# Fourteen of 32 attention units turn their first scores by transposing DMAs instead of multiplying queries and keys a second time

## The chip, the cores and the metric

The kernel is one program on one core of a Trainium2 chip. The core has TensorE (PE, which multiplies matrices; PEld is its loading of weights), VectorE (DVE), ScalarE (ACT), GpSimd (POOL) and SyncE (SP), which issues all DMAs; 16 DMA engines move the data. The metric is the device time of one execution, as the median of several runs. A change of less than about 0.3% can't be told from none here.

## The reference

Two attention layers over 2048 positions, 1024 columns and 32 heads of 32 are computed from separate inputs, and their outputs are put side by side. The change lies in the first (A), which goes over four segments of 512 positions: causal softmax attention inside a segment, plus a linear memory of the segments before, mixed by a gate.

```python
for s in range(N):
    qs, ks, vs = q[:, :, s], k[:, :, s], v[:, :, s]
    logits = jnp.einsum("bhqd,bhkd->bhqk", qs, ks) * scale + mask
    p = _softmax(logits, axis=-1)
    a_dot = jnp.einsum("bhqk,bhkd->bhqd", p, vs)
    pq = phi(qs)
    num = jnp.einsum("bhld,bhde->bhle", pq, M)
    den = jnp.einsum("bhld,bhd->bhl", pq, z)[..., None] + 1e-6
    o = g * (num / den) + (1.0 - g) * a_dot
    pk = phi(ks)
    M = M + jnp.einsum("bhld,bhle->bhde", pk, vs)
    z = z + jnp.einsum("bhld->bhd", pk)
```

The second layer (B) is a linear attention with two softmaxes as its feature map; the change leaves it as it is.

## The kernel before

**Tiling.** Layer A runs in 32 units, each one segment and one group of four heads (128 columns). `units` lists them: units 0 to 15 hold segments 0 and 1, units 16 to 31 segments 2 and 3. `produce(u)` projects keys and queries of a unit into PSUM (L420), splits them into two fp16 halves and copies these by six DMAs into an operand tile, in the program `st`, in the trace `S` (L872). `attend(u)` computes the attention. `values(u)` makes the values of two units. Numbers are held as a high and a low fp16 half, so most products are three matmuls or a stack of three along the contraction.

**A unit's attention before.** First, `maxima` multiplies queries (as rows) with keys for each head and each block of 128 queries, only up to the diagonal (L939). 16 products of 128 to 512 columns fill ten PSUM banks. DVE adds the causal mask and keeps the maximum of each row in `mt` (L945). These maxima are split into halves (L959, L962), turned by four small matmuls (L967), copied by ACT into rows 96 to 103 of the operand tile (L969), and spread to the other heads by a small DMA (L971). Second, `scores` multiplies keys (as rows) with queries over 104 contraction rows, so that the maximum of each query is subtracted in the product (L1032): 16 products in ten banks again. ACT takes the exponential of a bank at once (L1036), ACT and DVE write the two fp16 halves `ph` (L1038, L1039), and POOL sets to zero what lies above the diagonal (L1045). Third, `pv` multiplies these with the values, 20 short matmuls for each head in one group (L1068), and DVE adds the parts into `oall` (L1072). Last, the sums are divided and scaled into `osum` (L1091), the memory's part is added, PE transposes the result (L1100), ACT copies it to `oT` and a DMA stores it (L1102).

**Around it.** In the same stage, POOL, ACT and DVE prepare the second layer's weights (`fold`, L444 to L527), which are stored by L1127 through the buffers `fo` and `oT`, and other operands are loaded and stored. A kind of transposing DMA is there already: the key features of a unit, 128 x 1024 in fp16, are turned from `pkh` to `pkt` (L896), and in the last stage `kls` to `pt` (L1645).

**What sets the order.** Every operation is recorded with an engine, a planned duration, a priority and its tiles (`Graph.op`). `Graph.run` then places them one by one: it takes the engine that can start first, and there the ready operation of the lowest priority value, moved by a table of random offsets (`NUDGE`). DMAs are planned with a size in KB against one flow (`FLOW`, in KB per us) and a latency. The order of each engine is fixed by that when the program is built; on the chip each engine runs its list in order and waits where an operand is late. SP's list is in order too.

## Time and profile before

| | |
|---|---|
| median of 3 runs | 1672.32 us (1671.3 to 1675.79) |
| profiled execution, its own time | 1674.35 us |
| span of the profiled execution | 1672.4 us |
| PE busy | 1646.9 us (98%) |
| DVE busy | 1362.0 us (81%) |
| ACT busy | 1112.8 us (67%) |
| POOL busy | 1060.1 us (63%) |
| DMA engines | 55.8% of the span on SP's queue, 279.68 MB |

The profile is of one execution. Busy times are unions of an engine's instructions; PE's ends are modelled, so a matmul's length is longer than its step to the next one. In a group's row stand its busy time and the mean of one instruction, then the engine's idle time before them and what ended it. Slices are fortieths of the span, in tenths. The DMA share is the time that packets took, as a share of 16 engines; since packets can overlap on an engine, it can exceed 1.

### The profile page before, as it was taken

The page shows a single profiled execution, that of the slowest core. Times are in us where ns is not written, and L with a number is a line of the kernel's source. Part 1 is how long each engine was busy: PE and PEld are TensorE (multiplying, and loading weights), DVE is VectorE, ACT ScalarE, POOL GpSimd, SP SyncE. Part 2 cuts the span into 40 slices and gives each one's busy share as a digit, 9 for nine tenths or more (in the row PEclk, how much of TensorE's full clock was granted, in tenths as well). Part 3 has the DMA queues.
Part 4 walks back from the last instruction along what each step waited for, and adds up shares of the span by engine and source line. Part 5 has one row for each costly group of instructions (what it writes and reads, how often), then busy time and mean ns, then how long its engine had stood idle before and what let it go on. Part 6 is the DMA issues. An engine that isn't in the chain of part 4 may idle for free.

```text
span 1672.4 us, 35523 instructions
## 1 busy us (share of the span) xinstructions
PE 1646.9 (98%) x12900; PEld 963.9 (58%) x12900; DVE 1362.0 (81%) x3212; ACT 1112.8 (67%) x2044; POOL 1060.1 (63%) x1393
## 2 busy tenths in 40 slices
PE   8999999999999999999999999999999999999999
...
DMA  7745455769456472757467354276556666853311
GB/s 235 234 133 157 139 173 165 211 187 246 120 162 160 131 179 90 189 180 197 154 196 265 121 197 169 89 255 246 179 136 156 166 173 152 216 151 139 120 57 63
DMA packets 265455, 279.68 MB, mean 167 GB/s; under 512 B 162752, under 2 KB 215744, under 8 KB 256704
## 3 DMA queue, kind: packets, MB, share of 16 engines
q1 hardware_dynamic: 265280, 277.42, 55.8%
...
q14 instruction: 74, 0.61, 0.1%
...
## 4 chain that ended last, share of the span: by engine, by line
PE 58%; DVE 7%; ACT 3%; issue 2%; POOL 1%; DMA 0%; POOLq 0%; ACTq 0%; DVEq 0%
PE proj L616 14%; PE proj L420 11%; PE misc L420 10%; PE proj L1717 5%; PE s L616 3%; PE s L1717 2%; PE s L1032 2%; PE s L939 2%; PE pv L1068 2%; PE misc L616 2%; PE pv L1653 1%; PE misc L1717 1%; DVE mx L1318 1%; PE kv L1472 1%; DVE ph L1039 1%
## 5 line engine op out<-in xcount | busy, mean ns | idle before, releaser
L420 PE MATMUL proj<-S,S 128*128 128x512 f16 (+1 forms) x2304 | 496.5, 344 | 0.7 <-ACT S L447 0.2
L420 PEld LDWEIGHTS <-S 128*128 128x128 f16 x3072 | 289.0, 98 | 162.1 <-issue 3.4
L616 PE MATMUL proj<-S,S 128*128 128x512 f16 x1488 | 343.9, 380 | 9.8 <-ACT cs L622 8.3
L616 PEld LDWEIGHTS <-S 128*128 128x128 f16 x1968 | 187.4, 98 | 223.9 <-issue 12.1
L1045 POOL TENSOR_SCALAR_AFFINE_SELECT ph<-ph 128x256 f16<-128x256 f16 (+1 forms) x448 | 193.5, 454 | 111.2 <-DVE ph L1039 96.0
L1039 DVE SCALAR_TENSOR_TENSOR ph<-s,ph 128x512 f16<-128x512 f32 x320 | 208.8, 684 | 51.9 <-ACT ph L1038 47.6
L945 DVE CUSTOM_DVE_ANT_0 s<-s,causal 128x384 f32<-128x384 f32 (+3 forms) x512 | 241.3, 511 | 8.0 <-PE s L939 5.6
L1038 ACT ACTIVATE ph<-s 128x512 f16<-128x512 f32 x320 | 185.5, 647 | 0.7
L420 PE MATMUL misc<-S,ot 128*128 128x512 f16 x768 | 171.0, 379 | 0.0
L1325 ACT ACTIVATE e<-e,sk 128x256 f32<-128x256 f32 x256 | 114.5, 500 | 58.7 <-DVE e L1322 36.4
L420 PEld LDWEIGHTS <-ot 128*128 128x128 f16 x768 | 73.9, 98 | 88.3
L1036 ACT ACTIVATE s<-s,bdl 128x512 f32<-128x512 f32 x160 | 105.8, 702 | 22.0 <-PE s L1032 21.9
L1036 ACT ACTIVATE s<-s,bd 128x512 f32<-128x512 f32 x160 | 103.0, 689 | 23.6 <-PE s L1032 16.0
L1032 PE MATMUL s<-S 104*128 104x512 f16 (+3 forms) x512 | 113.8, 300 | 0.1
L939 PE MATMUL s<-S 96*128 96x512 f16 (+3 forms) x512 | 112.0, 299 | 0.7 <-DVE dm L992 0.3
L420 PE MATMUL proj<-wv,S 128*128 128x256 f16 x768 | 101.4, 273 | 0.0
L1068 PEld LDWEIGHTS <-ph 128*128 128x128 f16 x2560 | 89.0, 96 | 19.6 <-POOL ph L1045 1.3
L1622 POOL TENSOR_TENSOR e<-e,zb 128x512 f32<-128x512 f32 x64 | 84.9, 1340 | 16.6 <-DVE r L1328 13.5
L1068 PE MATMUL pv<-vl,ph 128*128 128x66 f16 (+1 forms) x2560 | 92.6, 184 | 0.6 <-POOL ph L1045 0.6
L1328 DVE TENSOR_REDUCE r<-e 128x32 f32<-128x1024 f32 x64 | 76.7, 1207 | 13.5 <-ACT e L1325 13.4
L616 PE MATMUL s<-S,S 128*128 128x512 f16 x324 | 78.6, 379 | 0.4 <-DVE S L449 0.4
L945 DVE DVE_READ_ACCUMULATOR2_ANT mt<- 128x1 f32 x512 | 72.4, 141 | 0.0
...
## 6 DMA issues: line engine op xcount, KB each, us to landing
S<-h SPq DMA_DIRECT2D x192, 128.0 KB
...
```

Of the source, the lines that this page charges most:

```text
L420: op(PE, dur, lambda c=c, a=a, b=b, lv=lv, rv=rv: nc.tensor.matmul(pv(), lv(), rv(), start=(c == 0 and a + b == 0), stop=(c == n - 1 and a ...
L616: op(PE, 0.2165, lambda n=n, a=a, b=b, lv=lv, rv=rv: nc.tensor.matmul(ps(), lv(), rv(), start=(start and n == 0 and a + b == 0), stop=(n = ...
L939: nc.tensor.matmul(ps()[:, o:o + 128 * i + 128], st()[0:96, 0, h, 128 * i:128 * i + 128], st()[0:96, 1, h, 0:128 * i + 128], start=True, s ...
L945: dve({128: 0.216, 256: 0.381, 384: 0.6, 512: 0.648}[n], lambda h=h, i=i, o=o, n=n: nc.vector.tensor_tensor_reduce(ps()[:, o:o + n], ps()[ ...
L1032: nc.tensor.matmul(ps()[:, o:o + n], st()[0:104, 1, h, 128 * j:128 * j + 128], st()[0:104, 0, h, 128 * j:512], start=True, stop=True)
L1036: act(0.571, lambda: nc.scalar.activation(ps(), ps(), AF.Exp, bias=0.0, scale=bd()[:, 4, i2, 0:1]), r=[(bd, i2)], w=[ps])
L1038: act(0.478, lambda: nc.scalar.activation(ph()[:, 0], ps(), AF.Copy, scale=2.0 ** 14), r=[ps], w=[(ph, 0)])
L1039: dve(0.6, lambda: nc.vector.scalar_tensor_tensor(ph()[:, 1], ps(), 2.0 ** 14, ph()[:, 0], op0=OP.mult, op1=OP.subtract), r=[ps, (ph, 0)], ...
L1045: nc.gpsimd.affine_select(pd, pd, pattern=[[0, n], [1, 128]], compare_op=OP.is_ge, fill=0.0, base=0, channel_multiplier=-1)
L1068: nc.tensor.matmul(ps()[:, i, n0:n1], ph()[:, a, o:o + 128], vl()[:, j, h4 + h, n0:n1], start=(i == 0 and a == 0), stop=(j == min(i, 2)), ...
L1325: op(ACT, 0.41, lambda i=i: nc.scalar.activation(e()[:, 4 * i:4 * i + 4], e()[:, 4 * i:4 * i + 4], AF.Exp, bias=0.0, scale=sk()[:, i:i + 1 ...
L1717: op(PE, 0.2165, lambda n=n, a=a, b=b: nc.tensor.matmul(ps(), v(a)[:, n, :], wform[w]()[:, b, n, :], start=(start and n == 0 and a + b == ...
```

## The change

For the units in `ROWS` (4 to 7, 12 to 15, 20 to 25) `maxima`, the turned maxima and `scores` are left out. In their place, `line` multiplies queries (as rows) with keys once. DVE adds the mask, multiplies by the negative scale of the logits, writes that back to PSUM and keeps the minimum of each row. ACT takes the exponential of each block with that minimum as its bias, so the mask needs no further step. ACT and DVE write the halves `ph`, and a transposing DMA turns both, 128 x 1024, into `pr`. `pvrow` multiplies one row of blocks with the values as soon as its transpose is there, so that a head's 20 matmuls are in up to four groups. A new entry of the bounds tile `bd` holds the negative scale. The other 18 units work as before, but their `ph` alternate between the buffers of `pr` and `ph`. `osum` is dropped: the scaled output is written to the buffer `oT`, in place. `FLOW` goes from 230 to 300, and the planned size of the old transposing DMA from 512 to 300. All of `NUDGE` is other numbers, so the order of every engine is new.

```diff
--- before.py
+++ after.py
@@ -30,6 +30,7 @@
 XS = (("S8", 4), ("S12", 3))
 XE = (("h3", 2), ("h3", 2), ("S15", 3))
 PVB = ((0, 1, 3, 2),)
+ROWS = (4,5,6,7,12,13,14,15,20,21,22,23,24,25)
 WSUB = ("DVE", "DVE", "DVE", "DVE")
 VLAG = 0.6
 XL = (5, -0.2)
@@ -43,22 +44,22 @@
-NUDGE = {0: 820989, 2: 102852, 3: 529656, 4: 266905, 5: 924189, 6: 435410, 9: 911235, 12: 450738, 13: 124130, 14: 669972,
...
+NUDGE = {0: 793787, 4: 392172, 5: 763851, 6: 686148, 8: 659744, 10: 367413, 11: 396531, 13: 340802, 14: 362282, 17: 982556,
...
@@ -112,7 +113,7 @@
            ("PE", "PE"): 0.0, ("POOL", "ACT"): 0.09, ("POOL", "DVE"): 0.08, ("POOL", "PE"): 0.16, ("POOL", "POOL"): 0.1}
 
     GAP, SHARE, WINDOW, filler = 0.5, 0.6, 3.41, None
-    SLACK, LATE, FLOW = 0.4, 1.5, 230.0
+    SLACK, LATE, FLOW = 0.4, 1.5, 300.0
     KEEP = {"proj": 1, "s": 1, "misc": 1, "pv": 1, "kv": 0}
     MOST = {"proj": 3, "s": 3, "misc": 2, "pv": 1, "kv": 4}
 
@@ -735,6 +736,8 @@
             bd()[:, 4, v, 0], ps()[:, v, 0], SCALE * 2.0 ** -12, bd()[:, 3, v, 1], op0=OP.mult, op1=OP.mult), r=[ps], w=w, prio=prio)
         op(DVE, 0.1, lambda: nc.vector.tensor_scalar(
             bd()[:, 5, v, 0], ps()[:, v, 1], 2.0 ** -14, 2.0 ** -14, op0=OP.mult, op1=OP.add), r=[ps], w=w, prio=prio)
+        op(POOL, 0.26, lambda: nc.gpsimd.tensor_scalar(
+            bd()[:, 4, v, 1], bd()[:, 4, v, 0], 1e-25, -1.0, op0=OP.max, op1=OP.mult), w=w, prio=prio)
         op(POOL, 0.18, lambda: nc.gpsimd.tensor_tensor(
             bd()[:, 0, v], xsc[:, s0:s0 + n, 0:1].to_broadcast([128, n, 2]), wgs[:, kk, :, 0][:, None, :].to_broadcast([128, n, 2]), op=OP.mult),
            r=[*((xscs, x) for x in segs), (wgss, (kk, 0)), (wgss, (kk, 1))], w=w, prio=prio)
@@ -795,6 +798,7 @@
             b(4, 0), ps()[:, :, :, 0], SCALE * 2.0 ** -12, b(3, 1), op0=OP.mult, op1=OP.mult), r=[ps], w=w, prio=prio)
         op(DVE, 0.12, lambda: nc.vector.tensor_scalar(
             b(5, 0), ps()[:, :, :, 1], 2.0 ** -14, 2.0 ** -14, op0=OP.mult, op1=OP.add), r=[ps], w=w, prio=prio)
+        op(POOL, 0.26, lambda: nc.gpsimd.tensor_scalar(b(4, 1), b(4, 0), 1e-25, -1.0, op0=OP.max, op1=OP.mult), w=w, prio=prio)
         op(DVE, 0.14, lambda: nc.vector.reciprocal(b(2), b(3)), w=w, prio=prio)
         op(DVE, 0.12, lambda: nc.vector.reciprocal(b(5, 1), b(5, 0)), w=w, prio=prio)
         for x in range(2):
@@ -893,9 +897,9 @@
                 op(POOL, 1.12, lambda p=p, ph=ph: nc.gpsimd.tensor_tensor(ph()[:, 1], p(), ph()[:, 0], op=OP.subtract),
                    r=[p, (ph, 0)], w=[(ph, 1)], prio=E)
                 d["pkt"] = pkt = G.buf("a", [128, 2, 4, 128], F16, "pkt", 1)
-                op(SP, 0.6, lambda ph=ph, pkt=pkt: nc.sync.dma_start_transpose(
+                op(SP, 1.3, lambda ph=ph, pkt=pkt: nc.sync.dma_start_transpose(
                     pkt().rearrange("p a j f -> p (a j) f"), ph().rearrange("p a t -> p (a t)")),
-                   r=[(ph, 0), (ph, 1)], w=[pkt], prio=E, lat=2.0, kb=512)
+                   r=[(ph, 0), (ph, 1)], w=[pkt], prio=E, lat=1.3, kb=300)
                 d["bdu"] = bdu = G.buf("a", [128, 4, 33], F32, "bdu", 2)
                 bv = d["bv"] = bvs[k // 2]
                 op(POOL, 0.426, lambda bdu=bdu, bv=bv: nc.gpsimd.tensor_scalar(
@@ -926,51 +930,52 @@
+        rows = u in ROWS
+        if not rows:
...
@@ -1034,7 +1039,7 @@
 
             pe(0.218, f, r=KR + QR + [(st, (1, 3, h)) for h in range(4)] + [(st, (0, 3 + h)) for h, _ in blocks], w=[ps])
             act(0.571, lambda: nc.scalar.activation(ps(), ps(), AF.Exp, bias=0.0, scale=bd()[:, 4, i2, 0:1]), r=[(bd, i2)], w=[ps])
-            ph = G.buf("a", [128, 2, 512], F16, "ph", 6)
+            ph = G.buf("a", [128, 2, 512], F16, *(("pr", 4), ("ph", 3))[len(pt) // 2 % 2])
             act(0.478, lambda: nc.scalar.activation(ph()[:, 0], ps(), AF.Copy, scale=2.0 ** 14), r=[ps], w=[(ph, 0)])
             dve(0.6, lambda: nc.vector.scalar_tensor_tensor(ph()[:, 1], ps(), 2.0 ** 14, ph()[:, 0], op0=OP.mult, op1=OP.subtract),
                 r=[ps, (ph, 0)], w=[(ph, 1)])
@@ -1073,17 +1078,91 @@
                 oall()[:, h], ps().rearrange("p c (t d) -> p c d t", t=2), axis=AX.X, op=OP.add),
                 r=[ps], w=[(oall, h)])
 
-        for a in (0, 2):
-            b = a + 1
-            scores([(a, 0)], (1, 1))
-            scores([(a, 1), (a, 3)], (3, 2))
-            scores([(a, 2), (b, 2)], (2, 2))
-            pv(a)
-            scores([(b, 0)], (1, 1))
-            scores([(b, 1), (b, 3)], (3, 2))
-            pv(b)
-
-        osum = G.buf("a", [128, 4, 128], F32, "osum", 1)
+        def line(*blocks):
+            ps = bank("s", [128, 512])
+            mx = G.buf("a", [128, 2], F32, "mr", 4)
+            at = []
+            for h, i in blocks:
+                at.append((h, i, at[-1][2] + 128 * at[-1][1] + 128 if at else 0))
+
+            def f():
+                for h, i, o in at:
+                    nc.tensor.matmul(ps()[:, o:o + 128 * i + 128], st()[0:96, 0, h, 128 * i:128 * i + 128],
+                                     st()[0:96, 1, h, 0:128 * i + 128], start=True, stop=True)
+
+            pe(0.108 * sum(i + 1 for _, i in blocks) / 2, f, r=KR + QR, w=[ps])
+            for k, (h, i, o) in enumerate(at):
+                n = 128 * i + 128
+                dve({128: 0.216, 256: 0.381, 384: 0.6, 512: 0.648}[n], lambda k=k, o=o, n=n: nc.vector.tensor_tensor_reduce(
+                    ps()[:, o:o + n], ps()[:, o:o + n], causal[:, 512 - n:512], bd()[:, 4, i2, 1:2], 3e38, OP.add, OP.min,
+                    mx()[:, k:k + 1]), r=[(bd, i2)], w=[(mx, k), (ps, k)])
+            for k, (h, i, o) in enumerate(at):
+                n = 128 * i + 128
+                act(0.2 + 0.00073 * n, lambda k=k, o=o, n=n: nc.scalar.activation(
+                    ps()[:, o:o + n], ps()[:, o:o + n], AF.Exp, bias=mx()[:, k:k + 1], scale=-1.0),
+                    r=[(mx, k)], w=[(ps, k)])
+            ph = G.buf("a", [128, 2, 512], F16, "ph", 3)
+            act(0.478, lambda: nc.scalar.activation(ph()[:, 0], ps(), AF.Copy, scale=2.0 ** 14), r=[ps], w=[(ph, 0)])
+            dve(0.6, lambda: nc.vector.scalar_tensor_tensor(ph()[:, 1], ps(), 2.0 ** 14, ph()[:, 0], op0=OP.mult, op1=OP.subtract),
+                r=[ps, (ph, 0)], w=[(ph, 1)])
+            pr = G.buf("a", [128, 2, 512], F16, "pr", 4)
+            op(SP, 1.3, lambda: nc.sync.dma_start_transpose(
+                pr().rearrange("p a (j f) -> p (a j) f", f=128), ph().rearrange("p a t -> p (a t)")),
+               r=[(ph, 0), (ph, 1)], w=[pr], prio=P, lat=1.3, kb=300)
+            for h, i, o in at:
+                pt[h, i] = pr, o
+
+        def pvrow(h, i, first):
+            if first:
+                pvs[h] = bank("pv", [128, 4, 66])
+            ps = pvs[h]
+            pr, o = pt[h, i]
+
+            def f():
+                for j in range(i + 1):
+                    for a, n0, n1 in ((1, 33, 66), (0, 0, 66)) if j == i else ((0, 0, 66), (1, 33, 66)):
+                        nc.tensor.matmul(ps()[:, i, n0:n1], pr()[:, a, o + 128 * j:o + 128 * j + 128], vl()[:, j, h4 + h, n0:n1],
+                                         start=(first and j == 0 and n0 == 0), stop=(j == i and a == 0), skip_group_check=True)
+
+            pe(0.06 * (i + 1), f, r=[pr, vl], w=[ps], short=True)
+
+        def pvsum(h):
+            ps = pvs[h]
+            dve(0.344, lambda: nc.vector.tensor_reduce(
+                oall()[:, h], ps().rearrange("p c (t d) -> p c d t", t=2), axis=AX.X, op=OP.add),
+                r=[ps], w=[(oall, h)])
+
+        pvs = {}
+        if rows:
+            for a in (0, 2):
+                b = a + 1
+                line((a, 3))
+                pvrow(a, 3, True)
+                line((a, 2), (a, 0))
+                pvrow(a, 2, False)
+                pvrow(a, 0, False)
+                line((a, 1), (b, 1))
+                pvrow(a, 1, False)
+                pvsum(a)
+                pvrow(b, 1, True)
+                line((b, 3))
+                pvrow(b, 3, False)
+                line((b, 2), (b, 0))
+                pvrow(b, 2, False)
+                pvrow(b, 0, False)
+                pvsum(b)
+        else:
+            for a in (0, 2):
+                b = a + 1
+                scores([(a, 0)], (1, 1))
+                scores([(a, 1), (a, 3)], (3, 2))
+                scores([(a, 2), (b, 2)], (2, 2))
+                pv(a)
+                scores([(b, 0)], (1, 1))
+                scores([(b, 1), (b, 3)], (3, 2))
+                pv(b)
+
+        osum = G.buf("a", [128, 4, 128], F32, "oT", 1)
         rd = G.buf("a", [128, 4, 4], F32, "rd", 1)
         dve(0.17, lambda: nc.vector.reciprocal(rd(), oall()[:, :, :, 32]), r=[oall], w=[rd])
         pool(0.174, lambda: nc.gpsimd.tensor_tensor(
@@ -1094,13 +1173,12 @@
         if s > 0:
             pool(1.23, lambda: nc.gpsimd.tensor_tensor(
                 osum(), osum(), amem().rearrange("p c h d -> p c (h d)"), op=OP.add), r=[amem, osum], w=[osum])
-        oT = G.buf("a", [128, 4, 128], F32, "oT", 1)
         po = bank("misc", [128, 4, 128], "output")
         for i in range(4):
-            pe(0.112, lambda i=i: nc.tensor.transpose(po()[:, i, :], osum()[:, i, :], ident), r=[osum], w=[po], need=[oT])
-        act(0.48, copy(oT, po), r=[po], w=[oT])
-        op(SP, 0.6, lambda: nc.sync.dma_start(oa_d[4 * s:4 * s + 4, :, g, :].rearrange("c p t -> p c t"), oT()),
-           r=[oT], w=[(osc, u)], prio=P, lat=1.5)
+            pe(0.112, lambda i=i: nc.tensor.transpose(po()[:, i, :], osum()[:, i, :], ident), r=[osum], w=[po])
+        act(0.48, copy(osum, po), r=[po], w=[osum])
+        op(SP, 0.6, lambda: nc.sync.dma_start(oa_d[4 * s:4 * s + 4, :, g, :].rearrange("c p t -> p c t"), osum()),
+           r=[osum], w=[(osc, u)], prio=P, lat=1.5)
 
     wfb, xfb, bob = (G.fixed(t) for t in (wf_d, xf_d, bo_d))
     lanes = [G.fixed(None) for _ in range(2)]
```

What the planner makes of it is seen in the orders. The first place is PE in unit 4 before, among the projections of values (L420); `S_127` is the unit's operand tile.

```order
L420 LDWEIGHTS S_763
L420 MATMUL proj<-S_1231,S_763 128x256
L1032 LDWEIGHTS S_127
L1032 MATMUL s<-S_127 128x256
L1032 LDWEIGHTS S_127
L1032 MATMUL s<-S_127 128x256
L420 LDWEIGHTS S_763
L420 MATMUL proj<-S_1231,S_763 128x256
```

The same engine in unit 4 of the change; L1178 is the transposing of an output, L1291 the fold of weights, L1124 the product with the values in `pvrow`.

```order
L421 LDWEIGHTS S_849
L421 MATMUL proj<-S_1382,S_849 128x256
L1178 MATMUL misc<-ident,oT 128x128 x4
L1291 MATMUL misc<-phib,st 128x128 x3
L1124 LDWEIGHTS pr
L1124 MATMUL pv<-vl_118,pr 128x66
L1124 LDWEIGHTS pr
L1124 MATMUL pv<-vl_118,pr 128x33
```

The second scores between the projections are gone; one row of blocks meets the values in a group of its own, whose weights are the transposed tile.

The second place is SP. Before, in unit 4 and the operands of those after it; the brackets hold the semaphores that the issue waits for (DMAHW are landings of earlier DMAs).

```order
L971 DMA S_127<-S_127 8x3x512 [waits Activation_49]
L872 DMA S_136<-h_2619 32x4x512 [waits DMAHW0_49,Activation_49]
L872 DMA S_136<-h_2619 32x4x512 [waits DMAHW1_49]
L896 DMA_TRANSPOSE pkt<-pkh 128x8x128 [waits DMAHW2_49,PE_49,Pool_49]
L1146 DMA st<-bwqk 128x512 [waits DMAHW3_49]
L1146 DMA st<-bwqk 128x512 [waits DMAHW4_49]
L467 DMA S_2791<-awv 128x2048 [waits DMAHW5_49,DVE_49]
L872 DMA S_136<-h_2619 32x4x512 [waits DMAHW6_49,DVE_49]
L872 DMA S_136<-h_2619 32x4x512 [waits DMAHW7_49,DVE_49]
L1127 DMA wf_d<-fo 1024x1x128 [waits DMAHW0_49,Pool_49]
L971 DMA S_147<-S_147 8x3x512 [waits DMAHW1_49,Activation_49]
L467 DMA S_3172<-aw 128x1024 [waits DMAHW5_49,DMAHW2_49,DVE_49]
```

SP in unit 5 of the change; L1109 is the transposing DMA of `line`, L876 and L900 are the L872 and L896 of before.

```order
L1109 DMA_TRANSPOSE pr<-ph 128x8x128 [waits DMAHW0_49,DVE_49,PE_49]
L876 DMA S_136<-h_3173 32x4x512 [waits DMAHW1_49]
L700 DMA wa_d<-S_1711 128x2048 [waits DMAHW2_49]
L700 DMA wa_d<-S_1711 128x2048 [waits DMAHW3_49]
L1109 DMA_TRANSPOSE pr<-ph 128x8x128 [waits DMAHW4_49,DVE_49,PE_49]
L1109 DMA_TRANSPOSE pr<-ph 128x8x128 [waits DMAHW5_49,DVE_49,PE_49]
L1109 DMA_TRANSPOSE pr<-ph 128x8x128 [waits DMAHW6_49,DVE_49,PE_49]
L900 DMA_TRANSPOSE pkt<-pkh 128x8x128 [waits DMAHW7_49,Pool_49]
L876 DMA S_136<-h_3173 32x4x512 [waits DMAHW0_49]
L876 DMA S_127<-h_3431 32x4x512 [waits DMAHW1_49,Activation_49]
L876 DMA S_127<-h_3431 32x4x512 [waits DMAHW2_49,DVE_49]
L1109 DMA_TRANSPOSE pr<-ph 128x8x128 [waits DMAHW3_49,DVE_49,PE_49]
```

The small DMA of the maxima (L971) is gone, and between the copies of the operands stand transposes that wait for DVE, and through PE for a free buffer.

74 lines of the change are left out of this document (37 added, 37 removed), and 30 rows, old and new, of the table NUDGE.

## The prediction

> **What bounds the kernel now.** I read the page first (busy shares, slices, the chain), then windows over the units that the change touches, then groups and the timeline of single engines.
>
> ```profile
> PE 1646.9 (98%) x12900; PEld 963.9 (58%) x12900; DVE 1362.0 (81%) x3212; ACT 1112.8 (67%) x2044; POOL 1060.1 (63%) x1393
> ...
> PE   8999999999999999999999999999999999999999
> ...
> DMA  7745455769456472757467354276556666853311
> ...
> PE 58%; DVE 7%; ACT 3%; issue 2%; POOL 1%; DMA 0%; POOLq 0%; ACTq 0%; DVEq 0%
> ```
>
> The rows are PE's busy time, its 40 slices, the DMA engines' slices and the chain's shares by engine. TensorE is busy 98% of the span, all along it, and the chain is mostly PE. The DMA engines are the uneven ones, from 3 to 9 tenths in the slices of the first half.
>
> The next view gives three stretches and the whole attention stage (busy us of PE, weight loads, DVE, ACT, POOL; then clock, DMA share, GB/s), and the row of the output's scaling, which runs once a unit.
>
> ```profile
> core 0: us, PE busy (x) PEld busy (x) DVE busy (x) ACT busy (x) POOL busy (x), PEclk, DMA share, GB/s
> 171.00:288.00 117.00, 116.86 (x1089) 80.37 (x1087) 109.11 (x324) 95.04 (x173) 77.12 (x120) 1.00 0.56 163
> 396.00:486.00 90.00, 89.65 (x858) 59.26 (x857) 78.57 (x228) 74.05 (x139) 70.63 (x105) 1.00 0.56 153
> 581.00:735.00 154.00, 153.87 (x1442) 103.99 (x1440) 129.11 (x388) 116.37 (x214) 119.81 (x171) 1.00 0.58 158
> 98.00:894.00 796.00, 791.71 (x7379) 530.78 (x7378) 694.06 (x2033) 627.14 (x1138) 592.69 (x873) 1.00 0.61 171
> ...
> L1091 DVE TENSOR_TENSOR osum<-oall,rd x32: 676/686/1634, 98.6 to 893.8; 128x512 f32<-128x512 f32 x32
> ```
>
> 32 starts from 98.6 to 893.8 make 25.65 us a unit. The three stretches lie between these starts for units 4 to 7, 12 to 15 and 20 to 25, the 14 that the change rewrites: 117 + 90 + 154 = 361 us. PE waits 0.6 us in all of them. So time taken from PE there is time gained, as long as nothing else becomes late; DVE (109.11 of 117 us in the first) and DMA (0.56 to 0.58) are the next to ask.
>
> **What PE loses and gains.** Since ends of matmuls are modelled, I price by starts.
>
> ```profile
> 456.17 0.71 PE L1068 MATMUL pv<-vl,ph 128*128 128x66 f16 x20
> 456.72 0.38 PE L939 MATMUL s<-S 96*128 96x384 f16 x2
> ...
> 457.38 0.60 PE L1032 MATMUL s<-S 104*128 104x512 f16 x3
> 457.81 0.60 PE L420 MATMUL proj<-S,S 128*128 128x512 f16 x2
> ...
> 462.29 2.11 PE L420 MATMUL proj<-S,S 128*128 128x512 f16 x9
> ...
> 653.03 0.39 PE L967 MATMUL misc<-identr,mh 128*8 128x128 f16 x4
> 653.35 1.92 PE L420 MATMUL proj<-wv,S 128*128 128x256 f16 x16
> ...
> 1062.09 0.53 PE L1472 MATMUL kv<-ot,pt 128*128 128x65 f16 x12
> 1062.45 0.81 PE L616 MATMUL proj<-S,S 128*128 128x512 f16 x3
> ```
>
> Three matmuls of the second scores (L1032) fill two banks of 512 columns from 457.38 to 457.81, and nine of 512 columns take 2.11 us, of which 0.38 is the length of the last: 0.216 us per 512 columns. A unit's second scores fill 10 banks: 2.16 us. The four matmuls that turn the maxima (L967) take 653.03 to 653.35, 0.32 us. Removed: 14 x 2.48 = 34.7 us.
>
> The product with the values stays at 80 matmuls a unit, but by the orders of both programs it stands in 231 groups instead of 128. A group of 20 takes 0.55 us (456.17 to 456.72), one of 12 in another stage 0.36 (1062.09 to 1062.45): 0.024 a matmul and 0.07 to 0.08 a group. At 0.075, 103 more groups cost 7.7 us. The lower bound is 0 (cost in proportion to matmuls); I take 7.7, as two rows fix it. PE's net: -27.0 us.
>
> **What the other engines get.** Groups by line (busy us, mean ns; then idle time before), and the durations of the operations on the maxima:
>
> ```profile
> L1039 DVE SCALAR_TENSOR_TENSOR ph<-s,ph 128x512 f16<-128x512 f32 x320 | 208.8, 684 | 51.9 <-ACT ph L1038 47.6 <-POOL sc L833 1.4 <-POOL ph L1045 1.3
> L1038 ACT ACTIVATE ph<-s 128x512 f16<-128x512 f32 x320 | 185.5, 647 | 0.7
> L1045 POOL TENSOR_SCALAR_AFFINE_SELECT ph<-ph 128x256 f16<-128x256 f16 x384 | 154.5, 422 | 82.1 <-DVE ph L1039 70.6 <-PE s L1032 3.0 <-DVE sif L433 1.4
> L1325 ACT ACTIVATE e<-e,sk 128x256 f32<-128x256 f32 x256 | 114.5, 500 | 58.7 <-DVE e L1322 36.4 <-DVE e L1320 17.1 <-DVE wsc L433 4.9
> L1036 ACT ACTIVATE s<-s,bd 128x512 f32<-128x512 f32 x160 | 103.0, 689 | 23.6 <-PE s L1032 16.0 <-DVE mt L945 7.5
> L945 DVE CUSTOM_DVE_ANT_0 s<-s,causal 128x512 f32<-128x512 f32 x128 | 90.6, 710 | 5.3 <-PE s L939 5.3
> L868 DVE SCALAR_TENSOR_TENSOR h<-proj,bd,h 128x512 f16<-128x512 f32 x32 | 23.7, 745 | 1.7 <-ACT h L866 1.1 <-ACT z L885 0.2 <-issue 0.2
> L969 ACT ACTIVATE S<-misc 8x512 f16<-8x512 f32 x32 | 18.7, 585 | 10.0 <-PE misc L967 9.2
> ...
> L959 DVE TENSOR_SCALAR_CACHE_REDUCE mh<-mt x32: 164/174/182, 54.3 to 866.6; 128x16 f16<-128x16 f32 x32
> L959 DVE DVE_READ_ACCUMULATOR mh<-mt x32: 77/84/92, 54.4 to 866.7; 128x1 f32 x32
> L962 DVE SCALAR_TENSOR_TENSOR mh<-mh,mt x32: 111/188/1224, 57.2 to 866.8; 128x16 f16<-128x16 f16 x32
> ```
>
> POOL loses 14 causal masks a unit (L1045, 12 of them 0.422 us): over 5 us, off the chain to the values as well. ACT trades 10 exponentials of 512 columns (0.689) and the maxima's copy (0.585) for 16 by blocks. 0.500 at 256 columns and 0.689 at 512 give 0.41 at 128 and 0.59 at 384: 4 x 2.19 = 8.8 us for 7.5, +1.3 a unit. DVE loses 0.174 + 0.084 + 0.188 and reads a scale per partition in 16 masked maxima; such an operand costs 0.745 - 0.684 = 0.06 (L868 against L1039): +0.5 a unit. The numbers to set against the stretches, 27 us shorter: ACT 285.5 + 18.2 of 334, covered; DVE 316.8 + 7 of 334, covered in sum, though in the first stretch 111 stand against 108 us. That is 0 to 3 us; I take 0, as its neighbours have room, and keep 3 for the range. The extra POOL operation on the bounds hides in the freed time. The scaled output now shares its buffer with the transposed one, so DVE could wait for a store; a unit's 24 us cover the few us of that, and I put it at 0.
>
> **What the DMA queue gets.** 140 transposes of 128 x 1024, and 14 small row copies fewer.
>
> ```profile
> 653.60 1.28 SPq L896 DMA_TRANSPOSE pkt<-pkh  x1
> ...
> 1497.41 5.56 SPq L1645 DMA_TRANSPOSE pt<-kls  x4
> 1503.06 1.01 SPq L1678 DMA_DIRECT2D e<-oa_d  x2
> ...
> 654.80:656.30 1.50, 1.50 (x15) 1.20 (x13) 0.54 (x1) 1.35 (x3) 1.50 (x1) 1.00 0.91 175
> 1281.60:1282.80 1.20, 1.20 (x7) 0.56 (x6) 1.20 (x3) 1.17 (x2) 1.04 (x4) 1.00 0.97 219
> 330.00:345.00 15.00, 15.00 (x132) 11.90 (x130) 11.46 (x38) 10.75 (x19) 7.48 (x12) 1.00 1.12 258
> ```
>
> The kernel already turns two fp16 halves of the same shape this way (L896), and others later (L1645). The first row is an issue, 1.28 us of SP; four in a row take 5.56, 1.39 each. The window from 654.80 holds nothing but that transpose: 175 GB/s for 1.5 us is its 262 KB, at a share of 0.91: 1.37 us of all 16 engines. A late one needs 1.16 (0.97 of 1.2 us). I take 1.37, the row with the same shape in the same stage.
>
> The engines' account over the three stretches: 117 x 0.56 + 90 x 0.56 + 154 x 0.58 = 205 us now; by the order the change issues 52.1 MB of other transfers there for 54.4: 197. With 140 x 1.37 = 192 that is 389 us, and 334 are to be had. If shares simply add, PE waits 55 us; at 1.16 a transpose, 25. But shares above one occur: 1.12 over 15 us at 330, with PE busy all the time. At 1.12 the 389 us pass in 347, so **13 us of waiting**; at 1.16, none. I take 13 and keep 0 and 55.
>
> Why would such lateness not show at once? Between a block's scores and its first use the order has at least 9.3 us (median 11.7) of other matmuls, at the starts above. The steps between take 0.71 + 0.69 + 0.65 + 0.68 and 2.7 from issue to the last packet (653.60 to 656.30): 5.4 us and the handovers. Some 3 us of lateness are covered, the rest is PE's. Queued behind a late transpose on SP are the copies of the next unit's scores operands, so a wait spreads.
>
> The sum, against the profiled execution's own 1674.35 us (span 1672.4): -34.7 + 7.7 + 13 = -14.0, so 1660.3. The median of the runs is 2.0 below that execution: **1658 us**.
>
> **The rivals.** *All transposes arrive in time* (1645 us): only PE's -27.0 counts. For it: the cover of 9.3 us, and the share of 1.12. Against it: the DMA engines have a slice of 9 tenths already. The Trainium skill, page "Advanced Engine Details and Errata", section "X-Bar Transpose (TRN2)", calls transposing DMAs as fast as regular ones and expects 350 to 400 GB/s. By that, an estimate, one would need 0.70 us and this rival would hold; the row's 175 GB/s is half of it and does not agree.
>
> *The DMA engines become the bound* (1700 us, slower): in the three stretches shares add and PE waits the full 55 us: 1674.35 - 27 + 55 - 2. It decides when the wait passes 27 us: when the engines pass less than 389 / 361 = 1.08 of their nominal time over a whole stretch, where 1.12 was seen over 15 us only. For it: the attention stage as a whole stands at 0.61, and the transposes come in bunches of four to six between other loads. Against it: a delay lets the same transfers spread. A second price may come on top:
>
> ```profile
> 55.00:59.00 4.00, 2.73 (x22) 2.24 (x20) 3.79 (x19) 3.76 (x8) 2.89 (x2) 1.00 1.02 294
> 59.00:67.00 8.00, 7.94 (x29) 3.86 (x28) 4.89 (x17) 6.78 (x12) 6.52 (x9) 0.57 0.64 162
> ```
>
> PE was busy 2.73 of 4 us, and the clock granted in the following 8 us was 0.57: 3.4 us lost. The Trainium skill, page "TensorE: Matmul & The Clock Gate", section "What's actually happening", says that the array's clock halves after an idle window of some 3.4 us. The trace agrees in kind, after gaps that were shorter. In this rival a few such drops would add 3 us each.
>
> *SP's queue gives the gain back* (1673 us): a unit needs 10 x 1.39 us for transposes and, by the order, 14 other issues at about 0.5 (two in 1.01 at 1503.06), 21 of 24 us, all in order, and each transpose waits for DVE. If a unit loses one transpose and one other issue to such a wait (2.0 us), 14 lose 28 us. For it: 90% load on one queue. Against it: the cover above.
>
> **How the numbers follow.** Forecast (10 to 20 us of DMA waiting, own range 1648 to 1667) 0.42; all in time 0.22; DMA bound 0.25; SP's queue 0.11. 0.3% is 5 us, about what a measurement of this kernel can tell. Faster is below 1667: 0.42 + 0.22 = 0.64. Same: 0.11. Slower: 0.25. The range goes from 1640 (PE's groups cost less than 7.7) to 1692, most of the DMA rival; beyond it, clock drops and longer transposes hold the rest.
>
> **What would show it.** Matmuls of the second scores 288 instead of 512, and the attention stage ending some 14 us earlier: the first step. DMA shares near or above 1.0 in the three stretches, with PE's idle time before the products with the values and before the first scores put down to DMA: the wait. If PE idles less than 3 us there, the first rival holds; if it idles over 27, or PEclk falls in a slice there, the second; if SP waits for DVE while the share is below 0.9, the third. A transposing issue far from 1.3 us, or 262 KB in other than 1.2 to 1.4 us, would prove the price wrong, and a DVE that PE waits for more than DMA would prove the bound wrong.

## The result and the profile after

| | before | after |
|---|---|---|
| median, in the same session | 1672.19 us (4 runs) | 1752.88 us (4 runs) |
| lowest to highest | 1671.3 to 1675.79 | 1744.36 to 1753.15 |
| ratio after / before | | 1.0466, 95% interval 1.0431 to 1.0501 |
| span of the profiled execution | 1672.4 | 1742.6 |

The change makes the kernel 80.7 us slower; 1658 was predicted, and 1692 was the upper end of the range. The profiled execution is the fastest of the four (1744.36 us), so the profile shows some 70 of the 81 us.

Page of the changed kernel: busy times, PE's and the DMA engines' slices, the chain of waits by engine.

```profile
PE 1646.4 (94%) x12636; PEld 941.4 (54%) x12636; DVE 1384.7 (79%) x3170; ACT 1128.4 (65%) x2114; POOL 978.8 (56%) x1208
...
PE   8999998999889988899989999999999999999999
...
DMA  7665999599995599998457435227745665565311
...
PE 39%; DVE 26%; DMA 12%; ACT 10%; POOL 6%; issue 5%; SPq 1%; DVEq 0%; ACTq 0%; POOLq 0%
```

The DMA slices show the three stretches with row units as bands of nines. PE has eights in half of them, where it had nines. The chain was 58% PE and is now 39%, with DVE at 26% (7% before) and DMA at 12% (0%). PE's idle time rose from 25.5 to 96.2 us (span less busy), while its busy time stayed, though the page counts 264 matmuls fewer. Its ends are modelled, so short waits can hide in it. The projections' group (busy us, mean ns; idle before, and what ended it), first of the kernel before, then of the changed one:

```profile
L420 PE MATMUL proj<-S,S 128*128 128x512 f16 (+1 forms) x2304 | 496.5, 344 | 0.7 <-ACT S L447 0.2 <-DVE ph L1039 0.2
```

```profile
L421 PE MATMUL proj<-S,S 128*128 128x512 f16 (+1 forms) x2304 | 505.2, 348 | 1.4 <-DVE ph L1106 0.6 <-DVE S L450 0.4 <-DVE amem L998 0.2
```

The same 2304 matmuls are 9 us longer in the second row, and only 1.4 us of idle time stand before them. Short waits or the lower clock can be in the 9 us; the row doesn't tell them apart.

The stretches of the 14 row units and the whole attention stage, by windows (columns as in the prediction: busy us of PE, weight loads, DVE, ACT, POOL, then clock, DMA share, GB/s):

```profile
181.00:290.00 109.00, 99.39 (x866) 61.65 (x866) 94.94 (x276) 82.58 (x165) 42.48 (x51) 0.97 1.14 228
411.00:513.00 102.00, 90.87 (x829) 56.36 (x827) 83.84 (x248) 73.52 (x146) 44.26 (x44) 1.00 1.15 212
606.00:791.00 185.00, 163.38 (x1417) 104.59 (x1415) 143.45 (x423) 127.71 (x250) 96.07 (x93) 0.97 1.12 224
86.50:943.60 857.10, 791.80 (x7132) 512.96 (x7130) 705.18 (x2012) 646.26 (x1209) 512.00 (x684) 0.99 0.88 201
```

PE waits 42 of these 396 us. By the trace, DVE ended 19.6 us of that and DMAs 17.1. The share is 1.12 to 1.15, about what 15 us in the kernel before showed with PE fully busy, but here it holds for 100 us and more and moves only 212 to 228 GB/s. The last row's end is the last unit's scaled output, 943.6 instead of 893.8.

The transposing line: its issues (ns, least, median, most), who waited for the transposes (us, times), and the time to landing.

```profile
L1109 SPq DMA_TRANSPOSE pr<-ph x140: 1231/1286/4646, 178.8 to 782.1; - x140
...
  ACT ph L1105: 37.3, 41
  PEld L1124: 26.9, 36
  PE pv L1124: 14.6, 22
DMA to landing us min/median/max: 3.1/4.2/6.4
```

ACT is held most: it can't write the next half before a transpose has freed one of the three `ph` buffers. DVE's low half then waits for ACT, as the page's rows of the two halves show (busy us, mean ns; idle before, and what ended it):

```profile
L1106 DVE SCALAR_TENSOR_TENSOR ph<-s,ph 128x512 f16<-128x512 f32 x140 | 95.3, 685 | 43.1 <-ACT ph L1105 42.9
L1105 ACT ACTIVATE ph<-s 128x512 f16<-128x512 f32 x140 | 83.1, 599 | 37.9 <-DMA pr<-ph 37.3
```

SP's own list in the middle stretch (start, us, instruction):

```profile
460.06 2.70 SPq L1109 DMA_TRANSPOSE pr<-ph  x2
462.81 2.25 SPq L900 DMA_TRANSPOSE pkt<-pkh  x1
465.17 2.65 SPq L1109 DMA_TRANSPOSE pr<-ph  x2
467.87 0.59 SPq L876 DMA_DIRECT2D S<-h  x1
468.57 1.26 SPq L1109 DMA_TRANSPOSE pr<-ph  x1
469.87 1.24 SPq L876 DMA_DIRECT2D S<-h  x2
471.23 2.68 SPq L1109 DMA_TRANSPOSE pr<-ph  x2
```

One issue follows the other within some 0.1 us. Nothing on SP waits in this window: its list is full.

### The profile page after: what moved, and what is told of

The parts are those of the page before. It is cut to its first block, busy times and chain, and to the rows that moved or that the text cites. A ratio compares the mean times of both kernels' runs of the same rounds, so it can differ in the third digit from the quotient of the medians.

```text
span 1742.6 us, 35004 instructions
## 1 busy us (share of the span) xinstructions
PE 1646.4 (94%) x12636; PEld 941.4 (54%) x12636; DVE 1384.7 (79%) x3170; ACT 1128.4 (65%) x2114; POOL 978.8 (56%) x1208
## 3 DMA queue, kind: packets, MB, share of 16 engines
q8 instruction: 99, 1.62, 0.4%
## 4 chain that ended last, share of the span: by engine, by line
PE 39%; DVE 26%; DMA 12%; ACT 10%; POOL 6%; issue 5%; SPq 1%; DVEq 0%; ACTq 0%; POOLq 0%
PE proj L617 9%; PE proj L421 7%; PE misc L421 6%; DMA pr<-ph 6%; PE proj L1795 5%; DVE S L450 3%; PE s L1795 2%; DVE s L951 2%; PE s L617 2%; ACT s L1041 2%; DVE s L1096 1%; DVE r L1406 1%; DVE pr L1044 1%; DVE mx L1396 1%; DVE ph L1106 1%
## 5 line engine op out<-in xcount | busy, mean ns | idle before, releaser
L951 DVE CUSTOM_DVE_ANT_0 s<-s,causal 128x128 f32<-128x128 f32 (+3 forms) x288 | 136.0, 509 | 9.2 <-PE s L945 7.8
L1101 ACT ACTIVATE s<-s,mr 128x512 f32<-128x512 f32 (+3 forms) x224 | 110.5, 505 | 36.0 <-DVE mr L1096 30.2
L1106 DVE SCALAR_TENSOR_TENSOR ph<-s,ph 128x512 f16<-128x512 f32 x140 | 95.3, 685 | 43.1 <-ACT ph L1105 42.9
L1105 ACT ACTIVATE ph<-s 128x512 f16<-128x512 f32 x140 | 83.1, 599 | 37.9 <-DMA pr<-ph 37.3
L1406 DVE TENSOR_REDUCE r<-e 128x32 f32<-128x1024 f32 x64 | 76.8, 1208 | 14.6 <-ACT e L1403 14.6
L1044 DVE SCALAR_TENSOR_TENSOR pr<-s,pr 128x512 f16<-128x512 f32 x108 | 72.1, 683 | 16.7 <-ACT pr L1043 16.4
L1050 POOL TENSOR_SCALAR_AFFINE_SELECT pr<-pr 128x256 f16<-128x256 f16 x144 | 59.9, 433 | 43.8 <-DVE pr L1044 33.4
L1124 PEld LDWEIGHTS <-pr 128*128 128x128 f16 x1120 | 51.2, 97 | 51.7 <-DMA pr<-ph 26.9
L1124 PE MATMUL pv<-vl,pr 128*128 128x66 f16 (+1 forms) x1120 | 58.4, 186 | 20.4 <-DMA pr<-ph 14.6
L1041 ACT ACTIVATE s<-s,bdl 128x512 f32<-128x512 f32 x100 | 66.5, 705 | 10.3 <-PE s L1037 10.2
L1543 POOL TENSOR_TENSOR pt<-e,pt 128x512 f16<-128x512 f32 x40 | 51.2, 1290 | 39.0 <-ACT pt L1540 39.0
L1096 DVE CUSTOM_DVE_ANT_0 s<-s,causal,bd 128x128 f32<-128x128 f32 (+3 forms) x128 | 68.7, 553 | 4.6 <-ACT s L1101 2.6
```

The source lines that it names most:

```text
L951: dve({128: 0.216, 256: 0.381, 384: 0.6, 512: 0.648}[n], lambda h=h, i=i, o=o, n=n: nc.vector.tensor_tensor_reduce(ps()[:, o:o + n], ps()[ ...
L1041: act(0.571, lambda: nc.scalar.activation(ps(), ps(), AF.Exp, bias=0.0, scale=bd()[:, 4, i2, 0:1]), r=[(bd, i2)], w=[ps])
L1044: dve(0.6, lambda: nc.vector.scalar_tensor_tensor(ph()[:, 1], ps(), 2.0 ** 14, ph()[:, 0], op0=OP.mult, op1=OP.subtract), r=[ps, (ph, 0)], ...
L1101: act(0.2 + 0.00073 * n, lambda k=k, o=o, n=n: nc.scalar.activation(ps()[:, o:o + n], ps()[:, o:o + n], AF.Exp, bias=mx()[:, k:k + 1], sca ...
L1106: dve(0.6, lambda: nc.vector.scalar_tensor_tensor(ph()[:, 1], ps(), 2.0 ** 14, ph()[:, 0], op0=OP.mult, op1=OP.subtract), r=[ps, (ph, 0)], ...
L1124: nc.tensor.matmul(ps()[:, i, n0:n1], pr()[:, a, o + 128 * j:o + 128 * j + 128], vl()[:, j, h4 + h, n0:n1], start=(first and j == 0 and n0 ...
```

## The experiments

Each run was compared with the kernel before on the same chip (1671.0 to 1672.3 us there). In what was expected, theory A says that the 16 DMA engines are full, B that the turned tile lands too late for the order and its three buffers, C that the new order itself costs, S that SP's queue is full.

### Transposes or order?

**e2_copy**: same order, waits and bytes, but nothing is turned.

```diff
-            op(SP, 1.3, lambda: nc.sync.dma_start_transpose(
-                pr().rearrange("p a (j f) -> p (a j) f", f=128), ph().rearrange("p a t -> p (a t)")),
+            op(SP, 1.3, lambda: nc.sync.dma_start(
+                pr().rearrange("p a t -> p (a t)"), ph().rearrange("p a t -> p (a t)")),
```

> Each of the 140 transposing DMAs becomes a plain copy of the same 128 x 1024 tile from and to the same buffers; order, waits and bytes are the same, the halves are not turned. Theory A: packets of 2 KB take the engines about half as long (some 0.7 us for 262 KB instead of 1.4 to 1.7), the share in the row stretches falls to 0.8 to 0.9 and most of the loss goes: 1660 us, between 1645 and 1685. Theory B: the copy still lands 2 us or more behind its issue, with the same three buffers; less than half of the loss goes: 1710 us or more.

Measured: 1710.16 us (ratio 1.0222, 1.0199 to 1.0246). Turning instead of copying costs 43 us, but 38 us above the kernel before remain, which theory A didn't expect. Theory B's number (1710 or more) is met, but by the next run 28 of the 38 us come without any landing. The line of the copies:

```profile
L1109 SPq DMA_DIRECT2D pr<-ph x140: 464/492/1649, 180.4 to 741.3; - x140
...
  ACT ph L1105: 9.0, 10
  PEld L1124: 2.9, 5
  PE pv L1124: 1.3, 4
DMA to landing us min/median/max: 2.3/3.6/9.0
```

A copy lands only 0.6 us earlier than a transpose (3.6 against 4.2), but its issue takes SP 0.49 us instead of 1.29.

**f2_none**: same order, no DMA at that place.

```diff
-        b = Buf(lambda: self.pools[pool].tile(shape, dtype, name=tag, tag=tag, bufs=bufs),
+        real, many = ("ph", 7) if tag in ("ph", "pr") else (tag, bufs)
+        b = Buf(lambda: self.pools[pool].tile(shape, dtype, name=real, tag=real, bufs=many),
...
-            op(SP, 1.3, lambda: nc.sync.dma_start_transpose(
-                pr().rearrange("p a (j f) -> p (a j) f", f=128), ph().rearrange("p a t -> p (a t)")),
+            op(SP, 1.3, lambda: None,
...
-                        nc.tensor.matmul(ps()[:, i, n0:n1], pr()[:, a, o + 128 * j:o + 128 * j + 128], vl()[:, j, h4 + h, n0:n1],
+                        nc.tensor.matmul(ps()[:, i, n0:n1], ph()[:, a, o + 128 * j:o + 128 * j + 128], vl()[:, j, h4 + h, n0:n1],
```

> The changed program in its own order without the 140 DMAs: the products with the values read the unturned halves from where they were written (7 buffers in all, as before), so there is neither load nor landing. If transposes alone make the loss (A and B together): 1645 to 1660 us. If the order itself, drawn with the planner's new figures, also costs (theory C; the plan without row units fell 35 us short of its chip time): 1685 to 1700 us. The difference to the plain copies (1710) is what their load and landing cost, the difference from there to 1753 what turning costs.

Measured: 1700.13 us (1.0172, 1.0157 to 1.0188). So the new order, with 14 units' second scores left out and no transposes at all, is still 28 us slower than the kernel before. Its three stretches by windows, and PE's longest wait for the row units (us, times, longest):

```profile
181.00:281.00 100.00, 94.75 (x864) 60.95 (x863) 93.44 (x276) 81.74 (x164) 42.43 (x50) 1.00 0.56 152
398.00:491.00 93.00, 89.06 (x837) 57.87 (x835) 83.24 (x249) 74.31 (x150) 44.24 (x44) 1.00 0.53 128
582.00:745.00 163.00, 155.37 (x1411) 102.73 (x1409) 140.97 (x422) 124.21 (x249) 95.42 (x92) 1.00 0.57 164
```

```profile
PE pv L1124 <- DVE ph L1107: 4.6, 8, 1.6
```

The DMA share is back at 0.53 to 0.57, yet PE waits 17 of 356 us, where the forecast started from 0.6. Counted over the trace, DVE ended 14 of the 17 us; it is busy 93 of 100 us in the first stretch. The attention stage's last output begins at 893.3 us, against 892.4 before, so nothing of the time taken from PE has been gained up to there; PE idles 37 us until then (11 before), 28 of them ended by DVE.

**e1_norow, f3_norow300, f4_norow230**: no row units at all. `e1` empties `ROWS` only, `f3` empties `NUDGE` too, `f4` also sets `FLOW` back.

```diff
-ROWS = (4,5,6,7,12,13,14,15,20,21,22,23,24,25)
+ROWS = ()
```

> The changed program with an empty list of row units: all 32 units go by columns, but the new order, the planner's new figures (FLOW 300, the old transpose at 1.3 us), the extra POOL operation and the 4 + 3 buffers for the halves stay. Theory A (the DMA engines are the bound in the row stretches) and theory B (the transposes' landing is too late for three buffers and the order): nothing of the loss is left, 1672 +- 12 us. Theory C (the new order and the buffers themselves cost): 1700 us or more.

> The changed program without row units and without the table of drawn numbers (NUDGE empty), planner's figure FLOW 300. Its own planner puts the end at 1713 us. Theory C1 (FLOW 300 lets loads be planned earlier than the engines bring them): 1740 us or more, and clearly above the next run. Theory C2 (only the draw of the order matters): equal to the next run within 10 us.

> As the run before with FLOW 230, the figure of the kernel before; the planner puts the end at 1718 us. C1: 1705 to 1725 us, 20 or more below the run with 300. C2: equal to it within 10 us.

Measured: 1766.77 (1.0549 to 1.0623), 1750.44 (1.0452 to 1.0489) and 1738.69 us (1.0383 to 1.0418). All units go by columns here, and the DMAs are the kernel before's: three other orders of nearly the same work cost 67 to 95 us. I had expected 1672 for `e1`; it is the clearest miss of the study. `FLOW` 300 against 230 makes 12 us between `f3` and `f4`, which falls between C1 and C2; the draw, the old transpose's planned figures, the small POOL operation and the other buffers were not tried apart.

**g2_later, g4_nonelater**: the numbers and the `FLOW` of the kernel before for all operations behind the attention stage, on the changed kernel and on `f2_none`.

```diff
+    if at >= FROM:
+        at += 45
+        seed = LATER.get(at // STRETCH, 0)
```

> The changed kernel with its row units as they are, but behind the attention stage the planner takes the drawn numbers and the FLOW of the kernel before (operations from number 9025 on, shifted by the 45 that are missing). The stages behind the attention stage took 780.0 us before and 802.1 after. Theory C (the later stages lost to their own new draw): they fall to 780 to 788 us, in all 1731 to 1740. Theory D (the attention stage hands its lateness on to them): 802 +- 4 us, no change.

> The order of the changed program without transposes (1700 us), the later stages with the draw of the kernel before. Theory C: 1678 to 1687 us, so that of the 28 us which this order lies above the kernel before some 18 are the later stages'. Theory D: 1700 us.

Measured: 1745.10 and 1696.81 us, 8 and 3 us less. From the start of the last unit's output (its `rd`) to the end the trace has 780.0 us before, 802.1 after, 796.8 in `g2`. So theory C holds for a small part. Counted by PE's starts, 47 matmuls of the later stages (10 us) that the order before carried into the attention stage now stand behind it.

### Engines, landing or queue?

**f1_load, g1_noneload, h4_moreload**: loads that nothing waits for. `f1` adds them to the kernel before, `g1` to `f2_none` where a transpose was, `h4` is `g1` with 1440 packets.

```diff
+                junk_n[0] += 1
+                nc.sync.dma_start(junk[junk_n[0] % 20][:, 0:64], aw[u % 8].rearrange("m p c f -> (m p c) f")[0:1024, 0:64])
```

> The kernel before, in its own order, with 140 more DMAs on SP's queue, one behind the lower half of each bank of scores in the 14 units: 256 KB from an input to a scratch tensor in DRAM, in 1024 packets of 256 bytes as a transpose has. Nothing waits for them and no buffer hangs on them. Theory A (the DMA engines' load delays all other transfers): the share in the three stretches goes to 1.0 or more and the time rises by 30 us or more, 1700 or above. Theory B (only what waits for the transposed tile itself is late): +10 us at the most, below 1683.

> The changed program's own order without the transposes (1700 us), and at the place of each transpose one of the DRAM loads that were tried in the order before (256 KB, 1024 packets of 256 bytes, 1.22 us of all engines each; nothing waits for them). Theory A (occupied engines delay all other transfers): the rise of 49 us that these loads brought in the order before comes here too: 1740 to 1755 us. Theory B (landing of the turned tile and the three buffers): 1700 to 1715 us.

> The run without transposes and with a DRAM load at each one's place (1708 us), the load made 1440 packets instead of 1024, which is 1.72 us of all engines each, what a transpose takes. Theory A (engines' time, whoever waits): 1735 to 1755 us. Theory L (the load alone does little, it is the wait for the turned tile's landing that costs): 1720 us or less.

Measured: `f1` 1719.65 us (1.0281 to 1.0316), +49. `g1` 1708.13 (1.0200 to 1.0235), only +8 on `f2_none`. `h4` 1757.82 (1.0494 to 1.0527), +58. `h4` in the same stretches, then `f1` in its own:

```profile
184.00:301.00 117.00, 99.06 (x865) 63.10 (x864) 94.80 (x275) 81.98 (x164) 42.38 (x50) 0.94 1.04 251
420.00:523.00 103.00, 92.15 (x832) 59.32 (x830) 83.72 (x249) 72.90 (x146) 44.29 (x44) 0.95 1.04 251
617.00:802.00 185.00, 163.13 (x1415) 107.27 (x1414) 142.88 (x423) 125.29 (x249) 95.46 (x92) 0.96 1.01 260
```

```profile
168.00:289.00 121.00, 114.94 (x1056) 78.44 (x1056) 104.99 (x310) 92.29 (x168) 71.85 (x114) 0.99 0.92 237
401.00:507.00 106.00, 94.35 (x878) 62.48 (x876) 79.75 (x239) 71.79 (x134) 72.33 (x108) 0.97 0.94 229
604.00:778.00 174.00, 159.47 (x1441) 106.03 (x1440) 129.53 (x388) 115.63 (x212) 120.55 (x170) 0.97 0.90 229
```

In `h4`, with nearly the engine time of the transposes (1.66 us a load, by its packets of 256 bytes, for 1.73) and no one waiting for the tile, the stretches last 405 us (396 in the changed kernel, 356 in `f2_none`). So a loss of this size needs no wait for a landing. But the share doesn't order the three runs: 8 us at 0.97, 58 at 1.03, and 49 at 0.92 in `f1`, where theory A had asked for 1.0 or more. Why the same load costs 49 us in the order before stays open; that order has no place on SP for these issues, which is an argument and no proof.

**g3_half**: every second transpose is a plain copy.

```diff
+            TURN[0] += 1
+            turned = TURN[0] % 2
```

> The changed program's order; every second of the 140 transposes is a plain copy, whose halves stay unturned. All copies gave 1710, all transposes 1753. Theory A with a limit that is passed (engines full only when nearly all are transposes): the cost is bent, 1720 us or less. A cost for each transpose, by landing or by engine time without a limit: half of the way, 1728 to 1735 us.

Measured: 1720.77 us (1.0276 to 1.0331). The first half of the transposes costs 11 us, the second 32: the cost is bent, as with a limit, and the time is at the bound set for theory A. The limit isn't a share of 1.0, since the share is already 1.06 here (table below).

**h2_issue, h5_issue1**: the plain copies with two (`h2`) or one (`h5`) DMA of 64 bytes behind each.

```diff
+                for _ in range(2):
+                    junk_n[0] += 1
+                    nc.sync.dma_start(junk[junk_n[0] % 40], aw[0, 0, 0:1, 0, 0:16])
```

> The plain copies (1710 us), each followed on SP's queue by two DMAs of 64 bytes from an input to DRAM scratch that nothing waits for: SP then issues 0.5 + 2 x 0.45 us, about what a transpose's issue takes, while the engines carry 0.75 us for a copy instead of 1.73. Theory S (SP's queue is the bound: its issues fill 0.89 of the row stretches in the changed kernel, 0.54 with copies): 1735 to 1755 us. Theory A (the engines): 1720 us or less.

> The plain copies (1710 us), each followed by one DMA of 64 bytes that nothing waits for, not two: 0.53 + 0.65 us and two handovers make SP's time for a tile about 1.25 us, what a transpose's issue takes when nothing else runs (1.28), while the engines stay near 0.85. If SP's time at that price is the bound (theory S), 1735 us or more. If it becomes one only through the issues that full engines hold up (1.62 us on average in the changed kernel) or with two small DMAs more, 1725 us or less.

Measured: `h5` 1734.97 us (1.0368 to 1.0405), 25 above the copies and at the limit set for theory S. ACT, PE's weight loads and PE wait some 45 us in all for the copies there, 13 in `e2`. `h2` 1846.79 (1.1027 to 1.1070), far beyond what was expected: a small DMA's issue took 0.65 us on average instead of 0.45, so SP needs 2.1 us a tile with handovers, where a transpose in the changed kernel needs 1.7. Its first stretch:

```profile
181.00:322.00 141.00, 108.53 (x868) 63.99 (x869) 96.33 (x276) 83.89 (x166) 42.71 (x51) 0.92 0.70 180
```

PE waits 32 of 141 us at a DMA share of 0.70: a full list on SP can hold the kernel up without full engines.

**h3_poolh**: the operand copies of the row units issued by POOL.

```diff
-                op(SP, 0.6, lambda r=r, i=i, m=m: nc.sync.dma_start(st()[32 * r:32 * r + 32, m], h3()[:, m, i, :]),
+                op(SP, 0.6, lambda r=r, i=i, m=m: (nc.gpsimd if u in ROWS else nc.sync).dma_start(st()[32 * r:32 * r + 32, m], h3()[:, m, i, :]),
```

> The changed kernel; in the 14 row units the six copies that lay out the operands of the scores are issued by POOL instead of SP, so that SP's issues in the row stretches fall from 0.89 to about 0.75 and those copies no longer queue behind transposes. The engines have the same work. Theory S: 1715 to 1735 us. Theory A: 1740 us or more. POOL has room (0.3 to 0.55 busy there), but what an issue costs it is not known.

Measured: 1775.29 us (1.0594 to 1.0640), slower than the change itself. POOL's list is in order too, so its masks now stand behind copies that wait for ACT and DVE, as PE's waits show (us, times, longest):

```profile
PE pv L1124 <- DMA pr<-ph: 25.1, 22, 3.0
PE pv L1073 <- POOL ph L1050: 9.2, 11, 2.7
```

With a new wait of 9.2 us for masks (nothing of the size was there before), the run tells nothing for or against S.

The runs in one table: over the three stretches (from the starts of `rd` of units 3, 11, 19 to those of 7, 15, 25), SP's issues summed, the time between issues that is under 0.3 us (handovers), what is left (SP free, in which SP may also wait for an operand), and the mean DMA share.

| run | stretches us | SP issues | handovers | SP free | share | median us |
|---|---|---|---|---|---|---|
| before | 358.9 | 138.2 | 10.9 | 209.8 | 0.58 | 1672 |
| f2_none | 356.2 | 122.9 | 10.3 | 222.3 | 0.56 | 1700 |
| g1_noneload | 363.5 | 294.6 | 20.1 | 48.6 | 0.97 | 1708 |
| e2_copy | 363.0 | 201.1 | 17.8 | 143.7 | 0.84 | 1710 |
| g3_half | 370.5 | 276.4 | 22.4 | 70.9 | 1.06 | 1721 |
| f1_load | 402.5 | 323.6 | 21.1 | 57.7 | 0.92 | 1720 |
| h5_issue1 | 385.1 | 302.3 | 33.9 | 48.9 | 0.81 | 1735 |
| after | 395.7 | 353.5 | 29.2 | 12.6 | 1.13 | 1753 |
| h4_moreload | 405.1 | 373.1 | 22.1 | 7.8 | 1.03 | 1758 |
| h2_issue | 500.0 | 409.9 | 41.6 | 48.1 | 0.69 | 1847 |

In the changed kernel SP is free 3% of the time, and its list holds up everything behind it. A transpose's issue, 1.28 us when nothing else runs, takes 1.62 there on average (224.5 us for 139). The issue of a load takes 0.88 us on average in `g1` and 1.16 in `h4`, with a least of 0.49 in both. That full engines hold the issues up fits these averages, but is not shown. The other DMAs of the changed kernel's stretches take no longer to issue than before (0.60 us for 0.59), and a transpose's issue behind 2 us at a share of 1.2 or more took 1.44 us on average (44 issues), one behind 0.8 to 1.0 took 1.69 (28). The Trainium skill, page "Perfetto Trace Analysis", section "DMA Instruction — HWDGE (DVE, Sync)", says that a profiled issue lasts until the descriptors are made and only then frees the sequencer. The rows agree in so far as the next issue starts only behind it, after some 0.1 us; what stretches an issue they don't show.

No column of the table orders the times alone. `g1` and `h5` leave SP the same 49 us, and lie 8 and 35 us above `f2_none`: in `h5` the products wait for the copies, in `g1` nothing waits for the loads. So where SP's list is nearly full, what waits for its DMAs counts too.

### Two tries that told little

**e3_spread** puts the row units at 5, 7, ... 31, and **e4_truth** gives the planner 3.0 us and 512 KB for a transpose.

```diff
-ROWS = (4,5,6,7,12,13,14,15,20,21,22,23,24,25)
+ROWS = (5,7,9,11,13,15,17,19,21,23,25,27,29,31)
```

> 14 row units again, but every second one from 5 to 31 instead of 4 to 7, 12 to 15 and 20 to 25; the planner makes a new order. Theory A: over two units the engines need about 25 us + 14 of transposes of 50 us, the share stays below 0.9, PE is not held up: 1665 us, 1645 to 1690. Theory B: each row unit costs what it costs now, about 5 us: 1740 us.

```diff
-               r=[(ph, 0), (ph, 1)], w=[pr], prio=P, lat=1.3, kb=300)
+               r=[(ph, 0), (ph, 1)], w=[pr], prio=P, lat=3.0, kb=512)
```

> The planner is told that a transpose takes 3.0 us behind its issue (now 1.3) and weighs 512 KB (now 300), so that it puts first uses and other loads later. Theory A: the engines stay full, the time falls by 20 us at the most: 1730 us or more. Theory B: the waits for a late transpose go: 1690 us or less.

Measured: 1802.87 (1.0759 to 1.0814) and 1835.11 us (1.0949 to 1.0993), both slower than the change itself, which no theory had foreseen. Both change what the planner places, so each runs in another order, and `e1` shows that this alone can cost 95 us. In `e3` SP has 139 us free in the units from 4 to 7, 12 to 15 and 20 to 25, and PE's weight loads still wait for turned tiles:

```profile
PEld L1124 <- DMA pr<-ph: 40.0, 45, 4.3
```

So landing may count in another order as well; that is left open.

No run beat the kernel before.

## Why the prediction was wrong, step by step

The miss is 1752.9 - 1658 = 95 us. It splits at `f2_none`: the rival "all in time" was to take 1645 us, the order without transposes took 1700 (55 us off), and transposes cost 53 us there instead of 13 (40 off).

**PE's net of -27.0 us: right.** Counted by starts in the trace of `f2_none`, the second scores fall from 71.9 to 40.2 us, the turned maxima from 10.5 to 5.9, and the product with the values rises from 73.0 to 76.8: 4 us instead of 7.7. That is -32.5; the first scores rise from 72.6 to 77.1, so -28.0 in all, with idle time behind a matmul counted to it. The second scores come to 288 matmuls, as said. It was not time gained, since PE then waited: the attention stage of the changed kernel ends 50 us later, not 14 earlier.

**"So time taken from PE there is time gained, as long as nothing else becomes late": the first step that failed (55 us).** PE's 0.6 us of waits in the three stretches belong to one order of four engine lists. The change draws another, and I priced that at nothing although the diff shows it. DVE, the first that I named to ask, became late: without any transpose it ended 14 of the 17 us that PE waits in the three stretches, where the sum had 0. By the two spans (1697.6 and 1672.4) `f2_none` loses 25 us, and 24 of them lie behind the attention stage, 10 by the moved matmuls. With the same columns work, three other orders cost 67 to 95 us more. What each of `FLOW`, draw, buffers and the fuller DVE has in the 55 is settled only for `FLOW` (some 12 without row units) and the later stages' draw (3 to 8).

**The engines' account: the second.** I priced a transpose at 1.37 us, and the packets of 256 bytes took 1.73 us a transpose (439.7 us of 16 engines after, 197.8 before, over 140). A ceiling of 1.12, read from 15 us, was taken as work that passes. Over 100 us it did not hold as one: above `f2_none`, the changed kernel at 1.13 loses 53 us, `h4` at 1.03 loses 58 and `g3` at 1.06 loses 21. The rival *the DMA engines become the bound* named this place, with 389 us of transfers for 334. It lacked the order's 55, and that its 55 meets the 53 measured is luck in part: its price was too low, and SP's list, which is in the 53, was not in its sum. The section "X-Bar Transpose (TRN2)" of the Trainium skill's page "Advanced Engine Details and Errata" (350 to 400 GB/s) is further off under load: 262 KB in 1.73 us are 151 GB/s.

**SP's queue: the third, and in the same 40 us.** "21 of 24 us" took other issues at 0.5, from a tight pair. The row of the operand copies in the trace of before has more:

```profile
L872 SPq DMA_DIRECT2D S<-h x192: 547/580/2246, 32.8 to 838.0; - x192
```

With the issues as they stood in the stretches (138 us for 220, less some 10 for 14 that go), 0.1 us of handover each (22) and 140 x 1.38, the sum is 343 us for the 334 to be had. So by the rows of before the queue would be full. Measured are 383 us. I also gave the wrong sign for it: SP was to wait for DVE at a share under 0.9, but a full queue waits for little (12.6 us without an issue).

How much of the 53 us is SP's and how much the engines' isn't settled. The runs give steps: a copy instead of nothing costs 10, SP's time at a transpose's own price 25 more (`h5`), and 18 are left for full engines and longer issues. That these add up is not shown, and `g1`, with SP's list as full as in `h5`, costs 8.

**Clock drops of about 3 us each: right in kind.** A window of 8 us behind one in which PE waited:

```profile
204.00:212.00 8.00, 6.95 (x59) 4.01 (x56) 6.36 (x23) 6.55 (x14) 2.83 (x6) 1.00 1.17 240
212.00:220.00 8.00, 7.51 (x37) 3.88 (x38) 6.49 (x21) 6.86 (x14) 3.00 (x3) 0.57 1.21 233
```

3.4 us are lost there. The trace has six such drops between the first and the last matmuls, 24 us at a granted clock of 0.5 (12 us lost); before it has two, 10 us (5 lost).

**DVE and ACT covered, POOL free:** the sums are as said (DVE 318 us of the 356 in `f2_none`, 324 forecast), but the 0 taken for DVE stands against the 14 us of PE's waits that it ended there. In the changed kernel it ended more of them than the DMAs (19.6 and 17.1 us), which was the sign named for a wrong bound. Some of that is the transposes' again, by way of ACT's 37.3 us for their buffers.
